# Sliding-window attention feeding a token mixer on one core: row sums for two steps, one predicated copy for two heads, and longer distances behind the scores

## The chip, the core and the metric

One core of a Trainium2 chip runs the whole kernel. The metric is the device time of one execution in microseconds (us). Engines are named as in the profile: PE (TensorE; its weight loads are PEld), DVE (VectorE), ACT (ScalarE), POOL (GpSimd) and SP (SyncE, which here only issues DMAs).

## The reference, cut to what matters

Three layers follow one another, on 4 batches of 768 tokens and 512 channels. The change lies in the first, attention with 8 heads of 64, 4 sink tokens and a window of 128:

```
scores = (q @ k.T) / 8                       # q, k, v: [4, 8, 768, 64]
keep   = (key < 4) or (0 <= query - key < 128)
a      = exp(scores - rowmax), 0 where not kept
a      = a / (sum(a) + 1e-9)
x      = a @ v                               # [4, 768, 512]
theta  = x @ w_theta
y      = w_tok_r @ (x cos theta) + w_tok_i @ (x sin theta)
u      = x + y;  u = u + relu(u @ w_ch)
out    = (sigmoid(causal 5-tap conv of u) * (u @ w_val)) @ w_out
```

## The kernel before, in words

**Tiling.** The queries are cut into blocks of 128 tokens: 6 a batch, 24 in all, here called groups (`g`, also `x` in the step functions; `i = g % 6` is the block within its batch). Heads go in pairs, 4 pairs to a block (`p`). One pair of one block is a step, `t = 4 g + p`, so there are `NT` = 96 steps. In the trace the eight score matmuls and weight loads of an even step belong to two steps, since `step_scores` issues steps `t` and `t + 1` together. A block needs only its own keys and the block's before, so the scores of a head are two pieces of 132 columns (128 keys and 4 sinks) in one PSUM bank.

**One step's way through the engines.** PE makes the scores (L428). DVE copies the keys of the block before over the masked half of the block's own (`copy_predicated`, L444, one for each head, none for the first block of a batch), then subtracts mask and takes the row maximum (L446, one for each head). ACT takes the exponential and the row sum (L452, one for each head). DVE adds eps to the two row sums of the step and inverts them (L461, L462), POOL multiplies the weights by that (L470). PE transposes the weights of two steps (L482, `weights_T`), ACT copies them out (L486), POOL cuts them by two triangles into the part for this block's values and the part for those of the block before (L493, L495). PE multiplies them with the values (L510, `attend`) and adds the sinks' part (L560, in `finish_x`). ACT copies the block's result to `uT` (L561) and rounds it to `xh` (L569); POOL makes the rest `xl` (L571); PE computes theta of the block from both (L101 to L103, 12 matmuls), and ACT copies it out (L584). The block's sink weights go a small way of their own (L526, L537, L543, L547, L551).

**The order** is written out by hand. The loop over `t` goes through the names of `ORDER` in each step; a name is a step function or a kind of deferred work that an earlier one put off with `later(kind, steps, f)`. What follows the scores does so at fixed distances:

```
LT, OX, OT = 4, 2 * NP, 4 * NP + 2        # NP = 4 head pairs
```

`LT` is how many steps after its scores a pair is transposed (`step_turn`), `OX` how many a block's `attend` and `finish_x` come after its first scores, `OT` the same for theta, half in each of two steps (`step_theta`). `split_x` comes 4 steps ahead of theta, and `keep_warm` issues a matmul on zeros in each step up to `OT`, which keeps PE occupied before theta begins. The loop ends `OT` steps after the last scores.

**Beside it run** the preparation of theta's weights (`wstages`, four blocks, one begun every four steps from step 0: DMA, ACT L133, POOL clamp L139, three joins on DVE L148, L151, L154, split by ACT L97 and POOL L98) and of the two token-mix matrices (12 jobs, one every 6 steps from step 18 on: the same operations, two transposes on DVE L236, and a DMA back to HBM). Keys and queries are loaded 8 steps ahead of a block's first scores; keys are transposed on PE 5 steps ahead, queries 4 (L393, copied out by ACT, L402). The first block of a batch also has its sink columns copied within `kT`, on DVE: `sink_keys(0)` (L410) and, a block later, `sink_keys(1)` (L412). The values of block `x` are loaded at step `4 x + TUNE['lv']` into one of three buffers, so that the load waits for `attend` of block `x - 2`. All DMAs are issued by SP, in order.

**PSUM** has 8 banks: `ps_s` (scores, four tiles of one bank, one for each head of two steps), `ps_t` 1, `ps_m` 2, `ps_h` 1 (`attend`, theta and keep-warm in turn).

After the last step the mixer's first steps (begun inside the last steps of the loop, at `turns`) go on with the token mix (L900 to L905), and then the channel layers (from L995) run to the end.

Of the kernel before, what the change touches and what calls it, by code (L numbers as in the profile page):

```python
# [9 lines left out]
F32 = mybir.dt.float32  # L10
# [4 lines left out]
ALU = mybir.AluOpType  # L15
AX = mybir.AxisListType
PSUM = bass.MemoryType.PSUM
DRAM = bass.MemoryType.DRAM

TUNE = dict(tc=0, xs=0, we=0, low=1, cut=1, xl=0, th=0, fx=0, nrm=0, w0=18, ll=8, lv=2, lq=4, lk=5, e=0, l2=0, ws=0, wp=4, bk=3, bq=3, bv=3, bqT=2, first=2, kw=4)  # L20
ORDER = ("range scale warm sinksT cut xl turn scores attend finish wth value wcopy scopy slow tcopy load "
         "softmax normalise low loads sink exp join sinks k sinkk q split theta qcopy fcopy thcopy fetch kcopy "
         "wturn ").split()
# [4 lines left out]
BIG = 3.0e38  # L28
# [7 lines left out]
def tile_sink_window_attention__then__token_mix__then__gated_conv(  # L36
# [16 lines left out]
    nc = tc.nc  # L53
    B, H, S, D = q.shape
    P = 128
    NP = H // 2
# [4 lines left out]
    SCALE = 1.0 / math.sqrt(D)  # L61
# [22 lines left out]
    th = {}  # L84
# [172 lines left out]
    def banded_attention(mixer):  # L257
        with ExitStack() as c0:
            pa = c0.enter_context(tc.tile_pool(name="pa", bufs=2))
            cq = c0.enter_context(ExitStack())  # L260
            pq = cq.enter_context(tc.tile_pool(name="pq", bufs=2, side="right"))
            ps_s = cq.enter_context(tc.tile_pool(name="ps_s", bufs=4, space=PSUM, side="right"))
            ps_t = c0.enter_context(tc.tile_pool(name="ps_t", bufs=1, space=PSUM))
            ps_m = c0.enter_context(tc.tile_pool(name="ps_m", bufs=2, space=PSUM))
            ps_h = c0.enter_context(tc.tile_pool(name="ps_h", bufs=1, space=PSUM))
# [1 line left out]
            ns = max(0, n_sink)  # L267
            ns += ns % 2
            KT = P + ns
            NR = 2 * NP * ns  # L270
            NSLOT = 3
            FIRST = TUNE['first']

# [8 lines left out]
            def later(kind, steps, f):  # L282
                defer.setdefault(kind, []).append((now[0] + steps, f))
# [16 lines left out]
            qn, kn, vn, qTs, vss, sms, pTs, sks, blks, xs, pss = ({} for _ in range(11))  # L300

            kT = pq.tile([P, NSLOT, NP, KT], F32, name="kT", bufs=1)
# [1 line left out]
            late = big.tile([P, 2, NQ * DM // 2], I32, tag=f"th{B - 1}", name="late")  # L304
            room = [late[:, z, :] for z in range(2)]
            bmask = pa.tile([96, NP], F32, name="bmask", bufs=1)
            eps = pa.tile([P, 2], F32, name="eps", bufs=1)
            nc.gpsimd.memset(eps, 1.0e-9)

            def build_masks():  # L310
# [39 lines left out]
            def load(g, what):  # L350
                b, i = divmod(g, NQ)
                for src, d, nm, bufs in ((k, kn, "kn", TUNE["bk"]), (q, qn, "qn", TUNE["bq"]), (v, vn, "vn", TUNE["bv"])):
                    if nm[0] not in what:
# [8 lines left out]
            def load_first(pieces):  # L362
                ts = []
                for src, d, nm in ((k, kn, "kn"), (q, qn, "qn")):
                    d[0] = pq.tile([P, H, D], F32, tag=nm, name=nm, bufs=TUNE["b" + nm[0]])
                    ts.append((d[0], src))
# [21 lines left out]
            def qk_transpose(g, which, p0=0, p1=NP):  # L388
# [5 lines left out]
                if which == 0:  # L394
                    if p0 == 0:
                        qTs[g] = pq.tile([P, NP, P], F32, tag="qT", name="qT", bufs=TUNE["bqT"])
                    d = qTs[g][:, p0:p1, :]
# [3 lines left out]
                def copies():  # L401
                    copier(TUNE['e'] >> which & 1)(d, ps)  # L402
                    if p1 == NP and which == 1 and i == 0 and ns:
# [3 lines left out]

            def sink_keys(n):
                if n == 0:
                    nc.vector.tensor_copy(kT[:, 0, :, P:KT], kT[:, 0, :, 0:ns])  # L410
                else:
                    nc.vector.tensor_copy(kT[:, 1:NSLOT, :, P:KT], kT[:, 0:1, :, P:KT]  # L412
                                          .to_broadcast([P, NSLOT - 1, NP, ns]))


            def scores(t):
                g, p = divmod(t, NP)
                i = g % NQ
                if i == 0:
                    w = 2 * P  # L420
                    k2 = kT[:, 0:1, p, 0:P].to_broadcast([P, 2, P])
                else:
                    o = (i - 1) % NSLOT
                    w = 2 * KT
                    k2 = kT[:, o:o + 2, p, :] if o < NSLOT - 1 else kT[:, 0:NSLOT:NSLOT - 1, p, :]
                pss[t] = [ps_s.tile([P, 512], F32, tag="s", name="ps_s") for _ in range(2)]
                for h, d in enumerate(halves):
                    nc.tensor.matmul(pss[t][h][:, 0:w], qTs[g][d, p, :], k2[d], start=True, stop=True)  # L428

            def softmax(t):  # L430
                g, p = divmod(t, NP)
                i = g % NQ
                if p == 0:
                    sms[g] = (pa.tile([P, 2, NP, ns + P], F32, tag="sm", name="sm"),
                              pa.tile([P, 2, NP], F32, tag="nm", name="nm"),
                              pa.tile([P, 2, NP], F32, tag="rs", name="rs"))
                sm, nm, rs = sms[g]
                a = ns if i == 0 else 0
                m = masks[min(i, 2)][:, a:]
                heads = list(enumerate(pss.pop(t)))  # L440
                if i > 0:
                    take = (upto if i % NSLOT == 0 else upper).bitcast(I32)
                    for h, ps in heads:
                        nc.vector.copy_predicated(ps[:, KT:KT + P], take, ps[:, 0:P])  # L444
                for h, ps in heads:
                    nc.vector.tensor_tensor_reduce(sm[:, h, p, a:], ps[:, P:KT + P - a], m, -SCALE, BIG, ALU.add,  # L446
                                                   ALU.min, nm[:, h, p:p + 1])

                def exps():
                    for h in range(2):  # L450
                        x = sm[:, h, p, a:]
                        nc.scalar.activation(x, x, AF.Exp, bias=nm[:, h, p:p + 1], scale=-1.0,  # L452
                                             accum_out=rs[:, h, p:p + 1])

                later("exp", 0, exps)

            def normalise(t):
                g, p = divmod(t, NP)
                sm, nm, rs = sms[g]
                r = rs[:, :, p]  # L460
                nc.vector.tensor_tensor(r, r, eps, ALU.add)  # L461
                nc.vector.reciprocal(r, r)  # L462
                x = sm[:, :, p, ns:]

                def scale():
                    if TUNE['nrm'] >> p & 1:
                        for h in range(2):
                            nc.vector.tensor_scalar(x[:, h], x[:, h], rs[:, h, p:p + 1], None, ALU.mult)
                    else:
                        nc.gpsimd.tensor_tensor(x, x, rs[:, :, p:p + 1].to_broadcast([P, 2, P]), ALU.mult)  # L470

                later("scale", 0, scale)

# [111 lines left out]


            NT = NG * NP
            LT, OX, OT = 4, 2 * NP, 4 * NP + 2  # L590
            W0, WP = TUNE['w0'], 6
            turns = [NT + n for n in (1, 4, 6, 7, 9)]
            load_first(FIRST)
# [62 lines left out]
                    softmax(t)  # L656

            def step_normalise(t, g, p):
                if 1 <= t <= NT:
                    normalise(t - 1)  # L660

            def step_sinks(t, g, p):
                if p == 0 and 1 <= g <= NG:
# [4 lines left out]
                    sink_T(g - 1)  # L668

            def step_attend(t, g, p):  # L670
                if OX <= t < NT + OX and t % NP == 0:
                    attend((t - OX) // NP)

            def step_finish(t, g, p):
# [66 lines left out]
            for t in range(NT + OT):  # L741
                now[0] = t
                g, p = divmod(t, NP)
# [388 lines left out]
```

## Time and profile before

| | us |
|---|---|
| median of 3 runs | 685.65 (684.75 to 686.59) |
| the profiled execution's own time | 688.93 |
| its span, first to last instruction | 687.2 |
| PE busy in the span | 658.7 (96%) |
| DVE busy | 522.0 (76%) |
| POOL busy | 402.9 (59%) |
| ACT busy | 356.5 (52%) |
| PE's weight loads busy | 578.0 (84%) |

Durations come from the profiled execution. The windows view gives the busy time of each engine in stretches of the span; the timeline gives single instructions with start, duration and, in brackets, how long the engine idled before and what ended that; "lines" groups instructions by line, engine and shape with busy time, mean duration and idle time before; the chain is the work that ended last, followed back from the end. Matmuls are pipelined and their ends are modelled, so that a busy PE isn't always PE at its peak. PEclk is the clock granted to TensorE as a share of 2.4 GHz.

### The profile page before, as it was taken

To read this page: it belongs to the slowest core of one execution; us is meant where nothing else is said; L and a number is where in the kernel's file an instruction comes from. 1 tells how busy PE (TensorE), PEld (TensorE's weight loads), DVE (VectorE), ACT (ScalarE), POOL (GpSimd) and SP (SyncE) were. 2 spreads that over 40 slices of the span, in tenths; PEclk is the share of its full clock that TensorE was granted. 3 is DMA by queue.
4 is the path that set the end of the run, shared out by engine and by line. 5 is a ranking of instruction groups with operands and counts; after the bars stand their busy time and mean duration, and the time that the engine had idled before them with its cause. 6 is when DMAs were issued, how large, how long until landed. Compare 5 with 4: busy or idle time off the path is not lost.

```text
span 687.2 us, 12293 instructions
## 1 busy us (share of the span) xinstructions
PE 658.7 (96%) x4139; PEld 578.0 (84%) x4139; DVE 522.0 (76%) x1409; ACT 356.5 (52%) x967; POOL 402.9 (59%) x457
## 2 busy tenths in 40 slices
PE   7779999999999999999999999999999999999998
PEld 4557767677677677999999999999989989989997
DVE  3686899989978965955656677676889889889773
ACT  5668777786777758643534444443423323323222
POOL 5588788879878885433433444436756447447330
PEclk9899999999999999999999999999999999999999
DMA  7747667797777246000110111100000100110111
GB/s 188 168 94 137 132 148 176 140 191 165 144 150 146 55 132 200 1 1 28 35 46 17 47 31 46 47 32 31 1 31 17 47 31 16 47 38 9 47 46 47
DMA packets 104334, 53.34 MB, mean 78 GB/s; under 512 B 80592, under 2 KB 96208, under 8 KB 104272
## 3 DMA queue, kind: packets, MB, share of 16 engines
q1 hardware_dynamic: 104272, 52.56, 31.7%
q8 instruction: 33, 0.54, 0.3%
q14 instruction: 29, 0.24, 0.1%
HBM read 41.54 MB, written 11.01 MB: 76 GB/s over the span
## 4 chain that ended last, share of the span: by engine, by line
PE 65%; DVE 21%; ACT 4%; POOL 3%; issue 3%; DMA 2%; SPq 1%; DVEq 0%; ACTq 0%; POOLq 0%
PE ps_y L103 9%; PE ps_y L101 9%; PE ps_y L102 9%; PE ps_s L428 3%; PE ps_o L103 3%; DVE acc L1043 3%; PE ps_o L102 3%; PE ps_o L101 3%; DVE sm L446 3%; DVE wc L154 2%; PE ps_c L103 2%; PE ps_c L101 2%; PE ps_c L102 2%; DVE ps_s L444 2%; PE ps_v L101 2%
## 5 line engine op out<-in xcount | busy, mean ns | idle before, releaser
L98 POOL TENSOR_TENSOR zl<-cs,zh 128x512 fp32r<-128x512 f32 x48 | 65.5, 1365 | 94.8 <-ACT zh L97 79.4
L1043 DVE SCALAR_TENSOR_TENSOR acc<-x,cw,acc 128x384 f32<-128x384 f32 x128 | 106.6, 833 | 2.4
L452 ACT ACTIVATE sm<-sm,nm 128x132 f32<-128x132 f32 (+1 forms) x192 | 76.3, 400 | 35.9 <-DVE nm L446 35.8
L470 POOL TENSOR_TENSOR sm<-sm,rs 128x256 f32<-128x256 f32 x96 | 69.7, 727 | 32.6 <-ACT sm L452 22.3
L98 POOL TENSOR_TENSOR x2l<-x,x2h 128x384 fp32r<-128x384 f32 x32 | 39.2, 1225 | 55.4 <-ACT x2h L97 55.4
L97 ACT CAST zh<-cs 128x512 fp32r<-128x512 f32 x48 | 29.8, 622 | 77.0 <-DVE cs L888 67.3
L428 PE MATMUL ps_s<-kT,qT 64*128 64x264 f32 (+1 forms) x384 | 63.4, 427 | 5.1 <-DVE nm L446 5.1
L101 PE MATMUL ps_y<-wt0h,zh 128*128 128x384 f32 x192 | 68.3, 356 | 0.0
L103 PE MATMUL ps_y<-wt0h,zl 128*128 128x384 f32 x192 | 64.9, 338 | 1.6 <-POOL zl L98 1.5
L103 PE MATMUL ps_y<-wt1h,zl 128*128 128x384 f32 x192 | 64.6, 337 | 0.0
L102 PE MATMUL ps_y<-wt1l,zh 128*128 128x384 f32 x192 | 64.6, 336 | 0.0
L102 PE MATMUL ps_y<-wt0l,zh 128*128 128x384 f32 x192 | 64.5, 336 | 0.0
L101 PE MATMUL ps_y<-wt1h,zh 128*128 128x384 f32 x192 | 64.5, 336 | 0.0
L428 PEld LDWEIGHTS ps_s<-kT,qT 64*128 64x128 f32 x384 | 36.2, 193 | 21.1 <-issue 8.3
L446 DVE CUSTOM_DVE_ANT_0 sm<-ps_s,mask 128x132 f32<-128x132 f32 (+1 forms) x192 | 48.4, 288 | 4.5 <-PE ps_s L428 3.9
L98 POOL TENSOR_TENSOR gl<-acc,gh 128x384 fp32r<-128x384 f32 x28 | 33.7, 1203 | 22.4 <-ACT gh L97 22.4
L444 DVE COPY_PREDICATED ps_s<-upper,ps_s 128x128 f32<-128x128 int32 x128 | 30.9, 287 | 19.7 <-PE ps_s L428 19.3
L97 ACT CAST x2h<-x 128x384 fp32r<-128x384 f32 x32 | 16.4, 514 | 54.7 <-DVE x L1029 54.7
L101 PE MATMUL ps_v<-x2h,held 128*128 128x384 f32 x128 | 43.3, 338 | 0.0
L102 PE MATMUL ps_v<-x2l,held 128*128 128x384 f32 x128 | 43.3, 338 | 0.0
L103 PE MATMUL ps_v<-x2h,held 128*128 128x384 f32 x128 | 43.2, 338 | 0.0
L101 PE MATMUL ps_h<-wthh,xh 128*128 128x512 f32 x96 | 42.3, 440 | 0.0
(157 smaller groups left out, 1978.6 us busy)
## 6 DMA issues: line engine op xcount, KB each, us to landing
vn<-in_v_dram SPq DMA_DIRECT2D x24, 256.0 KB, 4.7
kn<-in_k_dram SPq DMA_DIRECT2D x23, 256.0 KB, 4.6
qn<-in_q_dram SPq DMA_DIRECT2D x23, 256.0 KB, 5.1
out_dram<-o SPq DMA_DIRECT2D x23, 256.0 KB, 2.0
late<-in_moe_w_tok_r_dram SPq DMA_DIRECT2D x24, 192.0 KB
late<-in_moe_w_tok_i_dram SPq DMA_DIRECT2D x24, 192.0 KB, 3.2
wTr<-wTe SPq DMA_DIRECT2D x24, 96.0 KB, 3.6
wTi<-wTe SPq DMA_DIRECT2D x24, 96.0 KB, 2.8
```

The lines of the kernel that those rows point to most:

```text
L97: nc.scalar.copy(dst_h, src)
L98: lo_engine.tensor_tensor(dst_l, src, dst_h.bitcast(F32), ALU.subtract)
L101: nc.tensor.matmul(ps, lhs[0], rhs[0], start=first, stop=False)
L102: nc.tensor.matmul(ps, lhs[0], rhs[1], start=False, stop=False)
L103: nc.tensor.matmul(ps, lhs[1], rhs[0], start=False, stop=last)
L154: nc.vector.scalar_tensor_tensor(ci, lo, 29, ci, ALU.logical_shift_right, ALU.bitwise_or)
L428: nc.tensor.matmul(pss[t][h][:, 0:w], qTs[g][d, p, :], k2[d], start=True, stop=True)
L444: nc.vector.copy_predicated(ps[:, KT:KT + P], take, ps[:, 0:P])
L446: nc.vector.tensor_tensor_reduce(sm[:, h, p, a:], ps[:, P:KT + P - a], m, -SCALE, BIG, ALU.add, ALU.min, nm[:, h, p:p + 1])
L452: nc.scalar.activation(x, x, AF.Exp, bias=nm[:, h, p:p + 1], scale=-1.0, accum_out=rs[:, h, p:p + 1])
L470: nc.gpsimd.tensor_tensor(x, x, rs[:, :, p:p + 1].to_broadcast([P, 2, P]), ALU.mult)
L1043: nc.vector.scalar_tensor_tensor(a, x2[:, e, z:z + TB], cw[:, e, z:z + 1], a, ALU.mult, ALU.add)
```

## The change

The row sums of two steps are inverted in one pair of DVE operations on even steps, and their weights scaled by one POOL operation. The score tile holds both heads in two banks (two such tiles, as many banks as before), and one predicated copy serves both, with the mask broadcast over the heads. The sink columns are copied by ACT. `LT` goes from 4 to 6, `OX` from 8 to 10, `OT` from 18 to 20, and the values' load from 2 to 4 steps behind a block's first scores. As `OX` is no longer a multiple of 4, `attend` falls on the third step of a group, where it fell on the first; theta on the first and second, where it fell on the third and fourth.

```diff
-TUNE = dict(..., lv=2, ...)
+TUNE = dict(..., lv=4, ...)
...
-            ps_s = cq.enter_context(tc.tile_pool(name="ps_s", bufs=4, space=PSUM, side="right"))
+            ps_s = cq.enter_context(tc.tile_pool(name="ps_s", bufs=2, space=PSUM, side="right"))
...
-            eps = pa.tile([P, 2], F32, name="eps", bufs=1)
+            eps = pa.tile([P, 2, 2], F32, name="eps", bufs=1)
...
-                    nc.vector.tensor_copy(kT[:, 0, :, P:KT], kT[:, 0, :, 0:ns])
+                    nc.scalar.copy(kT[:, 0, :, P:KT], kT[:, 0, :, 0:ns])
                 else:
-                    nc.vector.tensor_copy(kT[:, 1:NSLOT, :, P:KT], kT[:, 0:1, :, P:KT]
+                    nc.scalar.copy(kT[:, 1:NSLOT, :, P:KT], kT[:, 0:1, :, P:KT]
                                           .to_broadcast([P, NSLOT - 1, NP, ns]))
...
-                pss[t] = [ps_s.tile([P, 512], F32, tag="s", name="ps_s") for _ in range(2)]
+                pss[t] = ps_s.tile([P, 2, 512], F32, tag="s", name="ps_s")
                 for h, d in enumerate(halves):
-                    nc.tensor.matmul(pss[t][h][:, 0:w], qTs[g][d, p, :], k2[d], start=True, stop=True)
+                    nc.tensor.matmul(pss[t][:, h, 0:w], qTs[g][d, p, :], k2[d], start=True, stop=True)
...
-                    for h, ps in heads:
-                        nc.vector.copy_predicated(ps[:, KT:KT + P], take, ps[:, 0:P])
-                for h, ps in heads:
-                    nc.vector.tensor_tensor_reduce(sm[:, h, p, a:], ps[:, P:KT + P - a], m, -SCALE, BIG, ALU.add,
+                    nc.vector.copy_predicated(ps[:, :, KT:KT + P], take[:, None, :].to_broadcast([P, 2, P]), ps[:, :, 0:P])
+                for h in range(2):
+                    nc.vector.tensor_tensor_reduce(sm[:, h, p, a:], ps[:, h, P:KT + P - a], m, -SCALE, BIG, ALU.add,
                                                    ALU.min, nm[:, h, p:p + 1])
...
-                r = rs[:, :, p]
+                r = rs[:, :, p:p + 2]
                 nc.vector.tensor_tensor(r, r, eps, ALU.add)
                 nc.vector.reciprocal(r, r)
-                x = sm[:, :, p, ns:]
...
-                        nc.gpsimd.tensor_tensor(x, x, rs[:, :, p:p + 1].to_broadcast([P, 2, P]), ALU.mult)
...
+                x = sm[:, :, p:p + 2, ns:]
+                later("scale", 0, lambda: nc.gpsimd.tensor_tensor(x, x, r[:, :, :, None].to_broadcast([P, 2, 2, P]),
+                                                                  ALU.mult))
...
-            LT, OX, OT = 4, 2 * NP, 4 * NP + 2
+            LT, OX, OT = 6, 2 * NP + 2, 5 * NP
...
-                if 1 <= t <= NT:
-                    normalise(t - 1)
+                if 2 <= t <= NT and t % 2 == 0:
+                    normalise(t - 2)
...
-                if OX <= t < NT + OX and t % NP == 0:
+                if OX <= t < NT + OX and (t - OX) % NP == 0:
                     attend((t - OX) // NP)
```

## Rows read from the trace of the kernel before

**Rows 1.** Windows: us; busy us of PE, PEld, DVE, ACT, POOL; PEclk, DMA share, GB/s

```profile
24.56:59.05 34.49, 26.58 (x204) 18.75 (x204) 22.89 (x108) 23.05 (x78) 26.51 (x37) 0.95 0.63 131
...
59.05:239.15 180.10, 172.63 (x1347) 131.03 (x1346) 159.06 (x629) 136.00 (x440) 146.82 (x193) 0.99 0.69 142
239.15:267.01 27.86, 26.42 (x197) 20.41 (x196) 17.41 (x52) 17.45 (x46) 20.20 (x26) 1.00 0.57 181
267.01:687.00 419.99, 414.66 (x2313) 397.49 (x2311) 311.20 (x556) 166.28 (x362) 196.97 (x166) 1.00 0.10 32
126.54:137.90 11.36, 11.36 (x89) 8.83 (x87) 10.85 (x37) 8.74 (x29) 10.25 (x14) 1.00 0.63 136
137.97:147.29 9.32, 9.32 (x78) 7.34 (x77) 7.87 (x32) 6.55 (x22) 6.54 (x8) 1.00 0.81 158
186.00:188.00 2.00, 2.00 (x7) 1.50 (x6) 1.88 (x9) 1.60 (x8) 1.93 (x4) 0.50 0.72 158
```

**Rows 2.** The chain of waits, PE's pieces: start us, us, what

```profile
53.72 0.44 PE ps_t L482 x4
...
248.90 1.97 PE ps_x L510 x32
250.86 0.43 PE ps_x L560
```

**Rows 3.** Timeline of the head, 40 to 47 us, engines in order of time

```profile
40.47 0.59 ACT L561 COPY uT<-ps_x 128x512 f32<-128x512 f32 x1
...
41.79 1.27 POOL L98 TENSOR_TENSOR wthl<-wc,wthh 128x512 fp32r<-128x512 f32 x1
43.03 0.61 POOL L139 TENSOR_SCALAR wc<-wc 128x512 f32<-128x512 f32 x1
...
43.68 0.83 DVE L148 TENSOR_SCALAR wc<-wc 128x512 int32<-128x512 int32 x1 [2.93 <-POOL wc L139]
...
46.72 0.44 PE L482 MATMUL ps_t<-ident,sm 128*128 128x128 f32 x2 [1.97 <-POOL sm L470]
```

**Rows 4.** Waits, 0 to 270 us: us in total, times, longest us

```profile
PEld ps_t L482 <- POOL sm L470: 11.4, 10, 2.2
```

**Rows 5.** Lines by shape, DVE, 0 to 270 us

```profile
L444 DVE COPY_PREDICATED ps_s<-upper,ps_s 128x128 f32<-128x128 int32 x128 | 30.9, 287 | 19.7 <-PE ps_s L428 19.3
L461 DVE TENSOR_TENSOR rs<-rs,eps 128x2 f32<-128x2 f32 x96 | 29.6, 308 | 1.9 <-ACT sm L452 1.9
...
L462 DVE RECIPROCAL rs<-rs 128x2 f32<-128x2 f32 x96 | 16.2, 168 | 3.3
...
L410 DVE COPY kT<-kT 128x16 f32<-128x16 f32 x4 | 5.8, 1453 | 0.5 <-ACT kT L402 0.5
...
L888 DVE TENSOR_TENSOR cs<-cs,ps_n 128x512 f32<-128x512 f32 x2 | 1.4, 688 | 1.2 <-ACT cs L881 1.2
```

**Rows 6.** Timeline, DVE: two predicated copies, and two of the sink copies

```profile
118.45 0.46 DVE L444 COPY_PREDICATED ps_s<-upper,ps_s 128x128 f32<-128x128 int32 x2
...
120.10 2.74 DVE L410 COPY kT<-kT 128x16 f32<-128x16 f32 x1
...
180.34 2.74 DVE L410 COPY kT<-kT 128x16 f32<-128x16 f32 x1
```

**Rows 7.** Lines by shape, ACT and POOL

```profile
L543 ACT CAST skr<-ps_sk 96x128 fp32r<-96x128 f32 x20 | 5.0, 248 | 0.0
...
L571 POOL TENSOR_TENSOR xl<-uT,xh 128x512 fp32r<-128x512 f32 x18 | 22.9, 1273 | 0.0
```

**Rows 8.** The row sums' tile: duration ns least/median/most, first and last start

```profile
L461 DVE TENSOR_TENSOR rs<-rs,eps x96: 150/160/1182, 12.1 to 248.2; 128x2 f32<-128x2 f32 x96
...
L470 POOL TENSOR_TENSOR sm<-sm,rs x96: 605/616/1274, 12.6 to 251.2; 128x256 f32<-128x256 f32 x96
```

**Rows 9.** Timeline: the load of a block's keys on SP, its transposes on PE

```profile
138.07 0.49 SPq L360 DMA_DIRECT2D kn<-in_k_dram  x1
...
145.46 0.60 PE L393 MATMUL ps_qk<-ident,kn 128*128 128x128 f32 x4
```

**Rows 10.** DMA issues, 40 to 260 us: KB each, median us to landing

```profile
kn<-in_k_dram SPq DMA_DIRECT2D x18, 256.0 KB, 5.9
```

More of the change, by code (lines that the diff above doesn't have):

```diff
@@ L18 @@
 DRAM = bass.MemoryType.DRAM
-TUNE = dict(tc=0, xs=0, we=0, low=1, cut=1, xl=0, th=0, fx=0, nrm=0, w0=18, ll=8, lv=2, lq=4, lk=5, e=0, l2=0, ws=0, wp=4, bk=3, bq=3, bv=3, bqT=2, first=2, kw=4)
+TUNE = dict(tc=0, xs=0, we=0, low=1, cut=1, xl=0, th=0, fx=0, nrm=0, w0=18, ll=8, lv=4, lq=4, lk=5, e=0, l2=0, ws=0, wp=4, bk=3, bq=3, bv=3, bqT=2, first=2, kw=4)
 ORDER = ("range scale warm sinksT cut xl turn scores attend finish wth value wcopy scopy slow tcopy load "
@@ L439, in softmax @@
                 m = masks[min(i, 2)][:, a:]
-                heads = list(enumerate(pss.pop(t)))
+                ps = pss.pop(t)
                 if i > 0:
                     take = (upto if i % NSLOT == 0 else upper).bitcast(I32)
-                    for h, ps in heads:
-                        nc.vector.copy_predicated(ps[:, KT:KT + P], take, ps[:, 0:P])
-                for h, ps in heads:
-                    nc.vector.tensor_tensor_reduce(sm[:, h, p, a:], ps[:, P:KT + P - a], m, -SCALE, BIG, ALU.add,
+                    nc.vector.copy_predicated(ps[:, :, KT:KT + P], take[:, None, :].to_broadcast([P, 2, P]), ps[:, :, 0:P])
+                for h in range(2):
+                    nc.vector.tensor_tensor_reduce(sm[:, h, p, a:], ps[:, h, P:KT + P - a], m, -SCALE, BIG, ALU.add,
                                                    ALU.min, nm[:, h, p:p + 1])
@@ L459, in normalise @@
                 sm, nm, rs = sms[g]
-                r = rs[:, :, p]
+                r = rs[:, :, p:p + 2]
                 nc.vector.tensor_tensor(r, r, eps, ALU.add)
                 nc.vector.reciprocal(r, r)
-                x = sm[:, :, p, ns:]
[L465 to L469, printed above, removed]
-                        nc.gpsimd.tensor_tensor(x, x, rs[:, :, p:p + 1].to_broadcast([P, 2, P]), ALU.mult)
-                later("scale", 0, scale)
+                x = sm[:, :, p:p + 2, ns:]
+                later("scale", 0, lambda: nc.gpsimd.tensor_tensor(x, x, r[:, :, :, None].to_broadcast([P, 2, 2, P]),
+                                                                  ALU.mult))
             def weights_T(t):
```

## The prediction

> **What bounds the kernel now.** Start with the stretches of the windows view [rows 1]. From 267.01 us to the end TensorE (PE) is busy 414.66 of 419.99 us. The change touches nothing there, so its effect lies in the attention stage, 0 to 267 us. In the 18 groups whose scores open at 59.05 and 239.15 us, PE is busy 172.63 of 180.10 us, VectorE (DVE) 159.06, GpSimd (POOL) 146.82, ScalarE (ACT) 136.00. A group (four steps) takes 180.10/18 = 10.0 us there, and DVE works 159.06/18 = 8.84 us of it.
>
> Two stretches show what these means mix. From 137.97 to 147.29 PE has no gap: 9.32 of 9.32 us, DVE 7.87. That is PE's own time for a full group. From 126.54 to 137.90 a group takes 11.36 us with DVE at 10.85: there DVE sets the pace, and PE's "busy" is stretched by waiting. So PE and DVE take turns. If nothing but PE held the 18 groups they would need 18 x 9.32 = 167.8 us, less three groups that open a batch: 16 of 32 attention matmuls and one sink matmul fewer, about 1.97/2 + 0.43 = 1.4 us each by the chain's pieces [rows 2]. That is 163.6 us; what there is to gain here ends at 16.5 us.
>
> The head is another case. From 24.56 to 59.05 three groups take 34.49 us, 11.5 each, while PE is busy 26.58/3 = 8.86 and POOL 26.51/3 = 8.84 a group [rows 1]. No engine is full; a chain goes round [rows 3]: the copy of `uT` at 40.47 (ACT, behind the attention matmuls), the split of `wthl` at 41.79 and the clamp at 43.03 (POOL), L148 at 43.68 after DVE idled 2.93 us, softmax, and the second half of the weights' transposes (L482) at 46.72, after PE idled 1.97 us for POOL's scaling. The next scores follow at once. Over the stage PE's weight loads for L482 stood 11.4 us in 10 waits for POOL's L470 [rows 4].
>
> **Part by part.** *Row sums of two steps at once.* L461 and L462 go from 96 to 48 each. Their busy time is 29.6 + 16.2 = 45.8 us for 96 [rows 5], so 48 fewer take 22.9 us off DVE, 0.95 a group. The row sum is four numbers a partition, not two; I price that at nothing, since the mean of 308 ns is start-up and waiting.
>
> *One predicated copy for two heads.* L444 mean 287 ns, but two in a row take 0.46 us together, because they overlap [rows 6]. One of 256 elements isn't in the trace. From below: the PSUM-reading L888 takes 688 ns for 512 elements, so (688 - 287)/384 = 1.04 ns an element, and 287 + 128 x 1.04 = 421 ns. From above: two copies without overlap, 574 ns. I take 421, the same kind of PSUM read: 80 x (0.46 - 0.42) = 3 us off DVE; by the upper end 9 us onto it. The shared two-bank score tile frees both heads together, one reduction (0.29 us) later than the first head alone; the ring still holds two steps, so I cost that at nothing while DVE is ahead.
>
> *Sink columns to ACT.* L410 takes 5.8 us of DVE in four copies (L412, four more, is left out of the sum) [rows 5]; two of them, as at 120.10 and 180.34, ran 2.74 us for 16 columns [rows 6]. ACT gets the eight small copies, nearest row 248 ns [rows 7]: 2 us on an engine with 44 us free of 180. Soon after the copy at 180.34, from 186 to 188, PE's granted clock is 0.50, the lower level of 1.2 GHz [rows 1]; a stretch at half clock costs PE up to half of its length.
>
> *One scaling for two steps.* L470 from 96 to 48, on 512 columns. Its median for 256 is 616 ns [rows 8], a 512-column operation takes 1273 [rows 7]: 2 x 616 = 1232, so POOL neither gains nor loses. DVE sheds 22.9 + 3 + 5.8 = 32 us in all, about 1.4 a group: 8.84 goes to 7.45, under the 7.87 at which PE ran without a gap.
>
> Against this stands a rule. L461 has a mean of 308 ns and a median of 160 [rows 5, 8]: some stand much longer than their work, 96 x 0.148 = 14 us in all. The Trainium skill ("SBUF — State Buffer", Who interferes with whom) says that VectorE and GpSimd share a port pair, an exclusive lock held for a whole instruction. By it a scaling twice as long blocks up to twice as long, so that the 7 us of this that I count as gone could all stay on DVE, and 32 would be 25. The forecast keeps 32 and would be the same with 25 (0.3 us a group): the slack of 9.32 - 7.45 us holds it.
>
> *Distances 4, 8, 18 to 6, 10, 20.* A pair's scaling is now issued on step 3 after its first scores and transposed on step 6: three steps between them where there was one. The L482 wait goes. Attention matmuls move from a group's first step to its third, theta from third and fourth to first and second. So in the head the `uT` copy no longer stands ahead of ACT's split of theta's weights, and the chain above opens in two places. What is late next there is POOL (8.84) or PE (8.86). I take 9.4, half a microsecond above, for what rest the joins leave: 34.49 - 3 x 9.4 = 6.3 us off. The keep-warm matmuls run two steps longer, in time that PE idles. For the 18 groups I take 9.4 each, as three groups are short but joins still bunch: 180.1 - 169.2 = 10.9 us off.
>
> After the last scores PE has one attention group (1.97 + 0.43) and a set of transposes (0.44) more [rows 2]: 2.8 us. The stretch from 239.15 to 267.01 has 27.86 - 26.42 = 1.4 us without PE [rows 1]; data that come two steps sooner should fill 1.0. That gives 1.8 back. The mixing's first steps keep their places.
>
> *Queues.* On SyncE (SP) the value load moves from two steps after its group's first scores to four, and there stands directly ahead of the next keys' and queries' loads. It waits for attention matmuls that also moved by two, so the wait isn't longer; behind it are keys, queries and the token weights' fetches. POOL keeps its order.
>
> Sum: -6.3 - 10.9 + 1.8 = -15.4 us. The profiled execution took 688.93 us (span 687.2), 3.28 above the median of 685.65; 673.5 for it becomes 670.2 for the median.
>
> **Rivals.** *A, only the stalls go (19%).* If the head stays on POOL because `wthl`, clamp and cuts are still in one queue, and DVE's joins keep bunching, then what is sure is the two long sink copies (2.74 us each less some 0.25) and the spell of low clock behind one of them, 5 to 8 us: 679.
>
> *B, DVE was the bound all along (8%).* DVE's 88% and PE's weight loads at 131.03 of 180.10 (73%) speak for it [rows 1]; the gapless group at 9.32 speaks against. If PE's pipeline had that room, DVE's whole 32 us would come off: about 654. The Trainium skill's "Perfetto Trace Analysis" (Identifying the Most-Contended Engine) says just this, that matmul busy time misleads and weight-load share should be read; the trace agrees on the shares, not yet on the bound.
>
> *C, slower: the keys land late (7%).* Keys issued at 138.07 are transposed at 145.46, 7.4 us on; they land in a median of 5.9, a margin of 1.5 [rows 9, 10]. The lead shrinks with the groups to 7.4 x 9.4/10 = 7.0, and a value load directly ahead takes up to 0.256 MB / 142 GB/s = 1.8 us. Then keys come 0.7 us late, PE's queue stands in all of some 20 groups, and 14 us eat the gain. From 0.8 us late it decides, at 1.0 the kernel is at 690. Against it: other groups have leads of 8 us and more, as loads run ahead.
>
> *D, nothing to measure (6%).* The gain and the longer drain cancel: 685.
>
> **Numbers.** The forecast (60%) covers 663 to 677: the copy's upper end and groups at 9.6 make it smaller, groups at 9.2 and a head at 8.9 larger. The range that holds 8 in 10 goes from 659 (towards B) to 681 (A). A measurement of this kernel can tell 0.3%, 2 us. Forecast, A and B are faster: 0.87; D is same: 0.06; C slower: 0.07.
>
> **What would show it.** Right: L444 x80 near 420 ns; L461 x48; L482's wait for L470 gone; L148's wait for the clamp under 1 us; score openings from the sixth group to the last about 169 us apart; DVE under 80% there; no 0.5 clock after the head. Wrong: PE waiting for `kn` (C), head groups above 10.5 us (A), groups well under 9.3 (B), L444 above 550 ns.

## The result, and the profile after

The changed kernel takes 669.47 us, the median of four runs (668.57 to 671.25), against 685.2 (684.14 to 686.59) for the kernel before in the same session: a ratio of 0.9759, 95% interval 0.9737 to 0.9781 (the quotient of these two medians, 0.977, lies within it). The forecast was 670.0, between 659 and 681.

In the code after, line numbers are smaller: L444 is now L443, L446 L445, L452 L451, L461 and L462 are L460 and L461, L470 is L463, L482 is L474, L493 and L495 are L485 and L487, L510 is L502, L561 is L553.

First the page's line of busy time. DVE goes from 522.0 to 485.5 us and POOL from 402.9 to 394.5, while the work of PE is the same. Of its 10 us less some 3 can be the clock (an estimate from the mean granted clock of the two executions, 0.992 before and 0.997 after); the rest I put down to time in which it was called busy and waited.

```profile
PE 648.7 (97%) x4141; PEld 573.3 (86%) x4141; DVE 485.5 (73%) x1226; ACT 355.2 (53%) x975; POOL 394.5 (59%) x408
```

Then the windows view of the profile after, in the stretches of [rows 1] (us; busy us of PE, PEld, DVE, ACT, POOL; PEclk, DMA share, GB/s): the head, the 18 groups, the drain up to the first mixing matmul, and the mixing to the end.

```profile
22.30:53.16 30.86, 24.05 (x193) 16.46 (x194) 18.63 (x88) 22.32 (x78) 23.38 (x29) 0.94 0.61 135
53.16:218.64 165.48, 164.87 (x1348) 127.65 (x1347) 130.79 (x491) 135.08 (x446) 141.86 (x157) 1.00 0.77 156
218.64:250.80 32.16, 29.40 (x213) 22.99 (x212) 17.52 (x48) 21.02 (x53) 24.20 (x26) 1.00 0.52 164
250.80:668.50 417.70, 413.90 (x2313) 397.63 (x2311) 308.18 (x554) 163.64 (x357) 194.46 (x165) 1.00 0.10 32
```

In the 18 groups PE now has 0.61 us without work, where it had 7.47, and a group takes 9.19 us on the mean; DVE's share there fell from 88% to 79%. By stage, from the openings (first score matmul) of the groups:

| us | before | after | difference | forecast |
|---|---|---|---|---|
| start to opening of the first group | 6.5 | 7.0 | +0.5 | 0 |
| first two groups | 18.0 | 15.3 | -2.7 | 0 |
| head, three groups | 34.5 | 30.9 | -3.6 | -6.3 |
| 18 groups | 180.1 | 165.5 | -14.6 | -10.9 |
| last opening to first mixing matmul | 27.9 | 32.2 | +4.3 | +1.8 |
| mixing to the end | 420.2 | 417.8 | -2.4 | 0 |
| span | 687.2 | 668.6 | -18.6 | -15.4 |

These are the two profiled executions, and the one before ran 3.3 us above its median, the one after 0.9. Part of what separates them is the clock and not the schedule: granted were 0.91 in the first two groups before and 1.00 after, and 0.99 and 1.00 in the 18 groups.

The lines by shape of the profile after (busy us, mean ns, idle time before), up to 250 us: of DVE, then of POOL and of ACT, cut to what answers to [rows 5], [rows 7] and [rows 8].

```profile
L443 DVE COPY_PREDICATED ps_s<-upper,ps_s 128x256 f32<-128x256 int32 x64 | 27.0, 422 | 31.7 <-PE ps_s L428 31.3
L460 DVE TENSOR_TENSOR rs<-rs,eps 128x4 f32<-128x4 f32 x48 | 22.1, 461 | 1.5 <-ACT sm L451 1.5
...
L154 DVE SCALAR_TENSOR_TENSOR wc<-late,wc 128x768 int32<-128x768 int32 x12 | 15.2, 1270 | 0.0
...
L461 DVE RECIPROCAL rs<-rs 128x4 f32<-128x4 f32 x48 | 8.6, 179 | 1.7
```

```profile
L463 POOL TENSOR_TENSOR sm<-sm,rs 128x512 f32<-128x512 f32 x48 | 55.9, 1164 | 18.1 <-ACT sm L451 8.2 <-DVE rs L461 5.4 <-PE ps_x L502 4.6
```

```profile
L410 ACT COPY kT<-kT 128x16 f32<-128x16 f32 x4 | 0.8, 210 | 0.0
```

The copy for two heads takes 422 ns (421 forecast). DVE now idles 31.3 us ahead of it, waiting for PE's scores: DVE is ahead of PE, as wanted. The row sums take 22.1 + 8.6 = 30.7 us for 45.8, a saving of 15.1 and not of 22.9, since each row sum stands 461 ns where it stood 308. POOL's scaling fell from 96 x 727 ns = 69.7 us to 55.9. The waits view of the stage (us in total, times, longest) still has two that stand mostly in the head (6.5 of the 10.0 us below lie in its three groups, the rest before it), and L474's wait for POOL's scaling, 11.4 us in ten waits of the weight loads before [rows 4], is not among them any more:

```profile
DVE wc L148 <- POOL wc L139: 10.0, 4, 3.8
PE ps_warm L592 <- ACT uT L553: 5.9, 3, 2.7
```

### The profile page after: what moved, and what is told of

Read it like the earlier page. It is cut to its first block, busy times and chain, and to the rows that moved or that the text cites. A ratio compares the mean times of both kernels' runs of the same rounds, so it can differ in the third digit from the quotient of the medians.

```text
span 668.6 us, 11958 instructions
## 1 busy us (share of the span) xinstructions
PE 648.7 (97%) x4141; PEld 573.3 (86%) x4141; DVE 485.5 (73%) x1226; ACT 355.2 (53%) x975; POOL 394.5 (59%) x408
## 4 chain that ended last, share of the span: by engine, by line
PE 82%; DVE 8%; issue 3%; ACT 2%; POOL 2%; DMA 1%; SPq 1%; DVEq 0%; ACTq 0%; POOLq 0%
PE ps_y L103 10%; PE ps_y L101 10%; PE ps_y L102 10%; PE ps_s L428 6%; PE ps_x L502 5%; PE ps_o L103 3%; DVE acc L1035 3%; PE ps_o L102 3%; PE ps_o L101 3%; PE ps_h L101 3%; PE ps_qk L393 3%; PE ps_h L103 3%; PE ps_h L102 3%; PE ps_c L103 2%; PE ps_c L101 2%
## 5 line engine op out<-in xcount | busy, mean ns | idle before, releaser
L451 ACT ACTIVATE sm<-sm,nm 128x132 f32<-128x132 f32 (+1 forms) x192 | 76.2, 400 | 29.0 <-DVE nm L445 28.8
L463 POOL TENSOR_TENSOR sm<-sm,rs 128x512 f32<-128x512 f32 x48 | 55.9, 1164 | 18.1 <-ACT sm L451 8.2
L428 PE MATMUL ps_s<-kT,qT 64*128 64x264 f32 (+1 forms) x384 | 59.8, 423 | 4.1 <-DVE nm L445 3.1
L445 DVE CUSTOM_DVE_ANT_0 sm<-ps_s,mask 128x132 f32<-128x132 f32 (+1 forms) x192 | 48.9, 292 | 9.9 <-PE ps_s L428 5.0
L428 PEld LDWEIGHTS ps_s<-kT,qT 64*128 64x128 f32 x384 | 33.3, 191 | 19.6 <-issue 8.6
L443 DVE COPY_PREDICATED ps_s<-upper,ps_s 128x256 f32<-128x256 int32 x64 | 27.0, 422 | 31.7 <-PE ps_s L428 31.3
L880 DVE TENSOR_TENSOR cs<-cs,ps_n 128x512 f32<-128x512 f32 x48 | 32.7, 681 | 11.5 <-ACT cs L873 10.2
```

The lines of the kernel that those rows point to most:

```text
L428: nc.tensor.matmul(pss[t][:, h, 0:w], qTs[g][d, p, :], k2[d], start=True, stop=True)
L445: nc.vector.tensor_tensor_reduce(sm[:, h, p, a:], ps[:, h, P:KT + P - a], m, -SCALE, BIG, ALU.add, ALU.min, nm[:, h, p:p + 1])
L463: later("scale", 0, lambda: nc.gpsimd.tensor_tensor(x, x, r[:, :, :, None].to_broadcast([P, 2, 2, P]), ALU.mult))
L880: nc.vector.tensor_tensor(x, x, pn[:, None, :].to_broadcast([P, 2, HD]), ALU.mult)
```

## The experiments

Every run is given as its median and as its ratio to the kernel before on the same chip; ratios are what is compared. "The change" is the whole one at 0.9759.

### The parts alone: distances, row sums, sinks

**The distances alone**, in the kernel before:

```diff
-TUNE = dict(..., lv=2, ...)
+TUNE = dict(..., lv=4, ...)
...
-            LT, OX, OT = 4, 2 * NP, 4 * NP + 2
+            LT, OX, OT = 6, 2 * NP + 2, 5 * NP
...
-                if OX <= t < NT + OX and t % NP == 0:
+                if OX <= t < NT + OX and (t - OX) % NP == 0:
```

> The kernel before with distances 6, 10, 20 and the value load 4 steps behind, and nothing else changed: DVE keeps its 32 us. My theory: head about 4 us less, the 18 groups about 4 us less (no wait for POOL's scaling), the drain 4 us more: 678 to 683. If the distances did all of it: 668 to 671. If DVE's load did all of it: 685 to 689, the longer drain showing alone.

Measured: 677.44 us, 0.9878 (0.9860 to 0.9897), just under the range and about half of the gain. Waits of L482 for the scaling are no longer listed. The 18 groups take 172.2 us with DVE busy for 155.2 of them.

**The row sums alone**, with the scaling that belongs to them, in the kernel before:

```diff
-                r = rs[:, :, p]
+                r = rs[:, :, p:p + 2]
...
-                x = sm[:, :, p, ns:]
+                x = sm[:, :, p:p + 2, ns:]
...
-                if 1 <= t <= NT:
-                    normalise(t - 1)
+                if 2 <= t <= NT and t % 2 == 0:
+                    normalise(t - 2)
```

> The kernel before with row sums, reciprocal and scaling merged over two steps, at the old distances, and nothing else changed. DVE loses about 20 us of work, but the scaling of a pair, now of 1.05 us, stands one step ahead of its transposes. My theory: 3 to 7 us less, 678 to 682, with PE's wait for POOL's scaling larger than the 11.4 us of before. Rival (DVE's load was the bound): 670 to 674. Rival (the pair's scaling comes too late for the old distance): 686 or more.

Measured: 687.23 us, 1.0016 (1.0000 to 1.0031), as the second rival had it. DVE was relieved as hoped: row sums and reciprocals take 15.5 + 8.6 = 24.1 us for 45.8. The time did not move, since the relief came back elsewhere. The waits view of this kernel (us in total, times, longest):

```profile
PEld ps_t L482 <- POOL sm L470: 23.3, 23, 2.7
PE ps_t L482 <- POOL sm L470: 16.7, 16, 2.3
```

The first was 11.4 us in ten waits before [rows 4]. The first of the two steps now waits for the second before it is scaled, and a transpose four steps behind the scores comes too early for that.

**The change with the old distances**:

```diff
-TUNE = dict(..., lv=4, ...)
+TUNE = dict(..., lv=2, ...)
...
-            LT, OX, OT = 6, 2 * NP + 2, 5 * NP
+            LT, OX, OT = 4, 2 * NP, 4 * NP + 2
```

> The changed kernel with distances 4, 8, 18 and the value load 2 steps behind, as before; merged row sums, two-head copy and sink columns on ACT stay. My theory (DVE and the short distances both held the stage; each part gives some, the head's chain needs the distances): the 18 groups gain about 8 us, the head nothing, the drain does not grow: 676 to 680. If the distances did all of it: 684 to 686. If DVE's load did all of it: 668 to 671.

Measured: 689.2 us, 1.0042 (1.0019 to 1.0065): slower than before, which neither theory had. The waits view shows the same turn as in the run above:

```profile
PEld ps_t L474 <- POOL sm L463: 22.5, 21, 2.9
PE ps_t L474 <- POOL sm L463: 17.3, 15, 2.5
```

DVE was busy for only 126.73 of the 179.06 us of the 18 groups, less than in the changed kernel, and still they took as long as before. So it was not DVE's load alone that held them.

**The sinks alone**, in the kernel before:

```diff
-                    nc.vector.tensor_copy(kT[:, 0, :, P:KT], kT[:, 0, :, 0:ns])
+                    nc.scalar.copy(kT[:, 0, :, P:KT], kT[:, 0, :, 0:ns])
...
-                    nc.vector.tensor_copy(kT[:, 1:NSLOT, :, P:KT], kT[:, 0:1, :, P:KT]
+                    nc.scalar.copy(kT[:, 1:NSLOT, :, P:KT], kT[:, 0:1, :, P:KT]
```

> The kernel before with the sink columns copied by ACT and nothing else changed. My theory: the two copies of 2.74 us go, and with one of them the half-clock stretch near 186 us: 3 to 6 us less, 679 to 682. Rival (the long copies only stood where DVE would have waited for scores anyway): 684 to 686.

Measured: 683.85 us, 0.9958 (0.9943 to 0.9974), just under 3 us; the 18 groups go from 180.1 to 177.2. That is less than forecast, between the theory and the rival. Both copies of 2.74 us [rows 6] are gone, and the two groups they stood in, 12.97 and 11.38 us long before, take 10.20 and 10.23. The stretch at the lower clock behind the second is gone with it: granted is 1.00 over the 18 groups of this run.

**The change without merged row sums** (copy, sinks and distances stay):

```diff
-                r = rs[:, :, p:p + 2]
+                r = rs[:, :, p]
...
-                x = sm[:, :, p:p + 2, ns:]
+                x = sm[:, :, p, ns:]
...
-                if 2 <= t <= NT and t % 2 == 0:
-                    normalise(t - 2)
+                if 1 <= t <= NT:
+                    normalise(t - 1)
```

> The changed kernel with the row sums, the reciprocal and the scaling of every step by themselves again (96 of each, not 48); the one copy for two heads, the sink columns on ScalarE and the longer distances stay. Theory: with the distances in place the merged row sums pay what VectorE sheds by them, half or more of the 8 us that lie between the distances alone (677.4 us) and the whole change (669.5): 673.5 to 677. Rival 1: the two-head copy and the sinks bring all of it, the merge nothing: 669 to 671. Rival 2: the merge costs here too, as it did without the distances: under 668.5.

Measured: 680.89 us, 0.9914 (0.9901 to 0.9928), beyond every range: it is slower than the distances alone (0.9878). With the distances in place the merge is worth 0.9914 - 0.9759 = 1.55% of 685 us, 10.6 us, and the two-head copy and the sinks together, without the merge, cost some 2.5 us. In the windows view the 18 groups of the distances alone (first) and of this kernel (second) have almost the same DVE time, though the second has 6 us fewer copies, the sinks' among them, by the sum of its lines:

```profile
53.37:225.61 172.24, 168.14 (x1348) 129.36 (x1347) 155.18 (x625) 134.35 (x440) 147.90 (x193) 1.00 0.74 150
```

```profile
55.73:229.79 174.06, 167.77 (x1348) 127.11 (x1347) 154.12 (x560) 135.27 (x446) 147.76 (x193) 1.00 0.73 149
```

Two copies in a row overlapped before [rows 6], so that merging them takes little off the union. What costs the 2.5 us was not separated; that the shared score tile frees both heads only together is a guess.

The four corners (the copy and the sinks are in the three runs marked *):

| ratio to before | row sums of each step | row sums of two steps |
|---|---|---|
| distances 4, 8, 18 | 1 | 1.0016, and 1.0042* |
| distances 6, 10, 20 | 0.9878, and 0.9914* | 0.9759* |

The merge brings nothing at the old distances (no run separates the 1.0042 into its parts) and 10 us at the new ones, measured there with the copy and the sinks in place; distances and merge without these two were not run. So the distances work alone in part, and the merge only with them.

### Who sets the pace now

**Twice the copy.** In the change each predicated copy is issued a second time, on the same data:

```diff
                     nc.vector.copy_predicated(ps[:, :, KT:KT + P], ...)
+                    nc.vector.copy_predicated(ps[:, :, KT:KT + P], ...)
```

> The changed kernel with each two-head predicated copy issued twice (the same result): 80 more of 0.35 to 0.42 us, 28 to 34 us more work for DVE, which brings it back to the load of before at the new distances. My theory (PE sets the pace now, DVE has some 20% to spare, of which joins that bunch need a part): 674 to 680, as with the distances alone. Rival B of the prediction (DVE is the bound): 695 or more. If DVE's time were free altogether: 669 to 671.

Measured: 686.02 us, 0.9996 (0.9978 to 1.0013): 16 us dearer than the change, between the two expectations. The added copies take 27.4 + 6.9 = 34.3 us of DVE, so about half of what is added shows. The 18 groups:

```profile
57.25:234.02 176.77, 168.37 (x1348) 126.74 (x1347) 149.33 (x551) 135.64 (x446) 140.08 (x158) 1.00 0.71 146
```

Here 18.5 us more DVE time in the window (149.33 for 130.79) make it 11.3 us longer (176.77 for 165.48). The new distances do not make DVE's load free: the slack of the changed kernel is small. The second copy stands in the way from the scores to the row maximum as well, and this run doesn't separate that delay from the load.

**Less work for PE.** Theta without its third product (12 matmuls a block become 8), in the change and in the kernel before:

```diff
-                mm3(hps[g], [x[:, c, :] for x in x2], [w[c] for w in wth], c == 0, c == KC - 1)
+                nc.tensor.matmul(hps[g], x2[0][:, c, :], wth[0][c], start=c == 0, stop=False)
+                nc.tensor.matmul(hps[g], x2[0][:, c, :], wth[1][c], start=False, stop=c == KC - 1)
```

> The changed kernel without the third product of theta (the rounding rest of x times theta's weights): 96 matmuls of 0.23 us fewer, 22 us of PE's time, 0.93 us a group. My theory (PE is the bound of the 18 groups and of the drain): 14 to 20 us less than the changed kernel, 650 to 656. Rival (a chain through DVE and POOL is the bound): 664 or more.

> The kernel before without the third product of theta: the same 22 us of PE's time. My theory (before, PE sets the pace only in part of the groups, the rest is DVE and waits for POOL): 5 to 11 us less than before, 674 to 680. Rival (PE was the bound before as well): 14 us or more less, under 671.

Measured: in the change 666.5 us, 0.9708 (0.9678 to 0.9737), 3 us less; in the kernel before 680.36 us, 0.9904 (0.9873 to 0.9936), 5.5 less as expected. The first is a miss, and lies in the rival's range: PE has about 13 us less to do in the 18 groups (151.73 busy for 164.87), and they are only 4.3 us shorter. In the kernel before (second line) they are 4.6 us shorter, 175.51 for 180.10.

```profile
53.21:214.38 161.17, 151.73 (x1276) 113.59 (x1275) 136.01 (x490) 134.16 (x446) 142.53 (x158) 1.00 0.78 160
...
57.46:232.97 175.51, 161.92 (x1276) 117.32 (x1275) 162.42 (x628) 135.20 (x442) 147.92 (x194) 0.99 0.71 147
```

So PE sets the pace in the changed kernel only to a depth of 4 us. What stands behind it was not found out: in this window DVE is busy for 84%, POOL for 88%, and PE waits 1.8 us for keys. And the pair doesn't show that PE bounds the change more than the kernel before, since the 18 groups give the same in both; what tells the two apart is PE's time without work there, 7.47 us before and 0.61 after. In this run more relief of PE alone brought little.

### The head

**Split and clamp of theta's weights on DVE.** The waits for L139 were put down to POOL's queue, where the clamp stands behind the scaling, two cuts and the split of the block before. In the change:

```diff
-                w_clamp(job[1], nc.gpsimd)
+                w_clamp(job[1], nc.vector)
...
-            split(dst[0][c], dst[1][c], job[1][0], nc.gpsimd)
+            split(dst[0][c], dst[1][c], job[1][0], nc.vector if room is not None else nc.gpsimd)
```

> The changed kernel with the clamp and the rounding rest of theta's weights (four blocks, in the head) on DVE, not on POOL. My theory (in the head DVE still waits about 10 us for the clamp behind that split in POOL's queue, while DVE is busy 60%): the head's three groups shrink by 2 to 4 us, 665 to 668. Rival (the head is set by ACT behind PE's attention matmuls): 669 to 671. Rival (the split delays the softmax on DVE): 672 or more.

Measured: 676.47 us, 0.9855 (0.9824 to 0.9886), 6.6 us slower than the change, in the range of the second rival; the first two groups take 18.6 us for 15.3, the head 34.2 for 30.9, the 18 groups 165.5 as before. The timeline, DVE and ACT around one of the splits:

```profile
38.33 0.62 ACT L97 CAST wthh<-wc 128x512 fp32r<-128x512 f32 x1
...
38.98 1.14 DVE L98 TENSOR_TENSOR wthl<-wc,wthh 128x512 fp32r<-128x512 f32 x1 [1.50 <-ACT wthh L97]
40.04 0.85 DVE L139 TENSOR_SCALAR wc<-wc 128x512 f32<-128x512 f32 x1
40.81 0.41 DVE L443 COPY_PREDICATED ps_s<-upto,ps_s 128x256 f32<-128x256 int32 x1
```

The wait moved with the work: DVE now stands for ACT's rounding, and the softmax (L443) stands behind it. A faster engine for the clamp did not help; that it is the order in the queue is what the next run tests, with the engines left as they are.

**The joins one step later.** The clamp stays on POOL, and in the head one step without work is put between it and DVE's first join:

```diff
-        return [fetch, bits, join(0), join(1), join(2), parts]
+        return [fetch, bits] + [lambda: None] * light + [join(0), join(1), join(2), parts]
```

> The changed kernel, with one idle step between the clamp of theta's head weights and VectorE's first join while only a few groups run (the head). Theory: in the head VectorE stands about 10 us in four waits for the clamp, because the clamp lies behind the scaling and the cuts in GpSimd's queue; a join issued one step later lets the softmax of that step pass ahead of it, so the head gives 2 to 5 us back: 665 to 668 us against 669.5. Rival 1: the chain of the head then waits for theta itself or for the joins a step later, and the time stays: 669 to 671. Rival 2: joins bunch with the next group's, and the head gets longer: above 671.

Measured: 666.27 us, 0.9706 (0.9693 to 0.9719): a hit, and faster than the change with no overlap of the intervals. The windows and the waits of this kernel:

```profile
22.43:49.78 27.35, 22.63 (x193) 15.49 (x193) 22.02 (x88) 22.45 (x78) 22.98 (x28) 1.00 0.67 152
49.78:215.28 165.50, 164.69 (x1348) 127.66 (x1347) 131.02 (x491) 135.14 (x446) 142.19 (x158) 1.00 0.76 157
```

```profile
PE ps_qk L393 <- DMA kn<-in_k_dram: 3.9, 5, 2.9
PE ps_warm L592 <- ACT uT L553: 2.6, 3, 1.2
DVE wc L148 <- POOL wc L139: 2.0, 1, 2.0
```

The head is 3.5 us shorter with the same work, the wait for the clamp went from 10.0 to 2.0 us, and the 18 groups stay as they were. The granted clock in the head is 1.00 where it was 0.94, but that isn't the cause: the run with both edits, below, has 0.94 again and the same head, and among runs with a granted clock of 1.000 the change takes 668.6 us and this kernel 666.0. Of the 3.9 us for which PE waits for keys one wait of 2.9 lies ahead of the head.

**Keep-warm only up to the first attention matmuls.** A keep-warm matmul shares its bank with the sum that ACT copies to `uT`:

```diff
-                if t < OT + 1:
+                if t < OX:
```

> The changed kernel with its keep-warm matmuls only up to the step of the first attention matmuls, not up to the first output matmuls. Theory: in the head TensorE stands 2.5 and 2.7 us in its queue because a keep-warm matmul shares its output bank with the transposes that ScalarE still copies into uT; without it the head gives 1 to 4 us back: 665.5 to 668.5 us against 669.5. Rival 1: the next real instruction stands in the same place, for the same copy: 669 to 671. Rival 2: TensorE falls to the 0.5 clock in the gap and the scores behind it run at half speed: 671 to 675.

Measured: 668.62 us, 0.9740 (0.9726 to 0.9754), not told apart from the change: the intervals overlap, and the head takes 30.7 us for 30.9. The clamp's wait is the same 10.0 us, and with the later joins alone PE's stop behind the `uT` copy went from 5.9 to 2.6 us by itself: more than half of it hung on the first wait. The granted clock of the head is lower, 0.89, so the theory fell and the second rival showed in part.

**Both edits of the head:**

> The changed kernel with both edits of the head: the idle step ahead of the joins and the shorter keep-warm. Theory: two different waits of one stage, each of which can hide the other, so that the two together give at least the sum: 662 to 666 us against 669.5. Rival 1: one of them was the other's shadow, and the time is that of the better edit alone. Rival 2: the head is held by GpSimd's own work and nothing moves: 669 to 671.

Measured: 665.81 us, 0.9701 (0.9687 to 0.9714). The theory's range held the time, but its reason did not: the head takes 27.4 us, as with the later joins alone (at a granted clock of 0.94), and the intervals of the two overlap. It is the first rival: the one edit gives all. The later joins are the version to keep.

## Why the prediction was right, and where its terms were wrong

The forecast's own case happened, at 669.5 for 670.0. That it came so close is luck: errors of several us in its terms cancelled, and between the two profiled executions, on the first of which the sum was made, the gain was 18.6 us for 15.4.

**PE and DVE take turns, and PE's gapless group is what is left: held.** The 18 groups now run at 9.19 us each with 0.61 us of gaps in all; the floor worked out was 163.6 us, the stage took 165.5. In the slow group before, where DVE was busy for 10.85 us, that was not all its own work: L154 took 2.72 us there, at 130.81, and 0.94 at 85.33; it ran beside a row of POOL's operations, of which the section on DVE's relief has more. I had taken 9.4 a group for bunching joins; it is 3.7 us better (165.5 for 169.2). How near the next limit stands, some 4 us behind PE, the prediction did not see.

**"The L482 wait goes": held, and it was the distances that took it.** This carries more than I wrote. I costed the merged row sums and the distances as two savings that add up. By the runs the merge by itself is worth nothing (1.0016), since it doubles the very wait that the distances remove. DVE's relief counts only where PE is not waiting for the scaling.

**DVE's relief: the size held, the lines did not.** In the 18 groups DVE went from 159.06 to 130.79 us, 7.27 a group for the 7.45 forecast. Row sums gave 15.1 us over the stage for 22.9. What I had not counted made up for it: DVE's three joins of weights (L148, L151, L154, those of 768 columns) went from 48.8 to 37.5 us. Either half of the change does that alone, 38.5 with the merged row sums and 40.4 with the distances.

The term that was mis-sized is the time for which a row sum stands beyond its own work. The views of the tile `rs` (least, median, most in ns), of the merge alone, the distances alone and the change:

```profile
L461 DVE TENSOR_TENSOR rs<-rs,eps x48: 151/160/901, 13.4 to 246.9; 128x4 f32<-128x4 f32 x48
...
L461 DVE TENSOR_TENSOR rs<-rs,eps x96: 150/402/1072, 12.2 to 236.3; 128x2 f32<-128x2 f32 x96
...
L460 DVE TENSOR_TENSOR rs<-rs,eps x48: 157/350/1257, 13.5 to 229.0; 128x4 f32<-128x4 f32 x48
```

A row sum that nothing holds takes 160 ns. What goes beyond that:

| | row sums | us in all | beyond 160 ns each |
|---|---|---|---|
| before | 96 | 29.6 | 14.2 |
| the merge alone | 48 | 15.5 | 7.8 |
| the distances alone | 96 | 37.7 | 22.3 |
| the change | 48 | 22.1 | 14.4 |

So the merge does take off the 7 us that I counted as gone, although the scaling is longer, and the new distances put 7 to 8 us on. The timeline shows why. Of the 48 row sums of the change 28 take over 200 ns, and each of these ends within 0.03 us of the end of the POOL operation that ran when it began: 16 times `xl` (L563), 11 times `blk` (L543), once the split of theta's weights, never the scaling. One of them:

```profile
68.19 1.28 POOL L563 TENSOR_TENSOR xl<-uT,xh 128x512 fp32r<-128x512 f32 x1
...
68.64 0.85 DVE L460 TENSOR_TENSOR rs<-rs,eps 128x4 f32<-128x4 f32 x1
```

Before, 39 of 40 end so, but only four of them behind `xl` and six behind the scaling. The rule weighed there said that a scaling twice as long could hold the row sums up to twice as long; instead it counts which of POOL's operations a row sum meets. This agrees with the lock between the two engines of which the Trainium skill tells ("SBUF — State Buffer", Who interferes with whom), without the doubling that I had worked out from it.

**POOL "neither gains nor loses": wrong, by 13.8 us of its busy time.** I took the nearest 512-column row, 1273 ns, which writes another type; the scaling's median is 1047 ns, for 2 x 616 of two halves.

**The head: the step that failed.** "The chain above opens in two places" was right for the first, L482, and half right for the second: `uT` no longer stands ahead of the split's rounding, but L148's wait for the clamp, forecast under 1 us, stayed at 10.0 (11.0 before). The timeline of POOL and DVE after shows why:

```profile
35.02 1.04 POOL L463 TENSOR_TENSOR sm<-sm,rs 128x512 f32<-128x512 f32 x1
...
36.02 0.64 POOL L485 TENSOR_SCALAR_AFFINE_SELECT pp<-pc 128x512 f32<-128x512 f32 x1
...
36.72 0.64 POOL L487 TENSOR_SCALAR_AFFINE_SELECT pc<-pc 128x512 f32<-128x512 f32 x1
...
37.33 1.27 POOL L98 TENSOR_TENSOR wthl<-wc,wthh 128x512 fp32r<-128x512 f32 x1
...
38.58 0.61 POOL L139 TENSOR_SCALAR wc<-wc 128x512 f32<-128x512 f32 x1
...
39.22 0.43 DVE L148 TENSOR_SCALAR wc<-wc 128x512 int32<-128x512 int32 x1 [3.77 <-POOL wc L139]
39.56 0.42 DVE L443 COPY_PREDICATED ps_s<-upto,ps_s 128x256 f32<-128x256 int32 x1
```

Five operations without a gap, from 35.02 to 39.19, and DVE's softmax in line behind the join that needs the last one. I named POOL as what is late next but priced it by its busy time a group (8.84); its order was what counted. The experiment with later joins gives what the step had promised: 27.35 us for the forecast 28.2.

**The drain: mis-sized, and given back.** +4.3 us for +1.8: I had let data that come sooner fill 1.0 of the 1.4 us of gaps, while the gaps grew, from 27.86 - 26.42 = 1.4 us to 32.16 - 29.40 = 2.8. Priced at nothing were the mixing's first steps, which get 2.4 us shorter beside the longer drain, in every run with the new distances and the whole of theta (417.7 to 417.8 us), and the first two groups, 2.7 us shorter. One wait of 2.0 us of L482 for the scaling was there too, and so was a stretch at the lower clock (0.91 granted before, 1.00 after); the two were not separated.

**The rivals.** A (only the stalls go) fell for the 18 groups and was half right for the head. B (DVE was the bound all along) fell: at the old distances DVE's relief brings nothing, and now PE runs almost without a gap; that DVE stands close behind, the doubled copy shows. The rule beside it ("Perfetto Trace Analysis", Identifying the Most-Contended Engine, in the Trainium skill), to judge by weight loads and not by matmul busy time, would still leave PE a quarter of headroom in the 18 groups (127.65 of 165.48 us, 77%). Taking PE work away shortened them by 4.3 us, so PE was the bound there, though only just. C (keys late) did not come: PE waits 0.2 us for `kn` after, where it waited 1.1 before; it begins to show only with the later joins, 3.9 us. D (nothing to measure) fell with the gain.

## What to carry to other kernels

Merging two small operations makes the first one's result later by a step: look whether its consumer is so far behind that it does not notice, and move the consumer in the same edit, or the saving on the engine turns into a wait of the same size. Where engines take turns, price an edit only together with the wait that hides it, and try each half alone. And where an engine waits for another that is not full, read the order in that engine's queue: moving the waiting instruction a step later brought some 3 us, moving the work to the waiting engine cost 6.6.

## What the runs showed that was not expected

A small DVE operation can stand several times its own work without any semaphore: the row sum of 128 x 4 numbers took from 157 to 1257 ns, and the copy of 16 columns that took 2.74 us on DVE twice [rows 6] takes 210 ns on ACT. With the distances alone, still on DVE, it took 155 ns. The two long ones began while POOL ran and ended with the fifth of five POOL operations that followed one another with hardly a gap; for the one at 180.34, which ends at 183.08, the fifth is

```profile
182.41 0.65 POOL L493 TENSOR_SCALAR_AFFINE_SELECT pp<-pc 128x512 f32<-128x512 f32 x1
```

The L154 of 2.72 us at 130.81 began and stood beside such a row of POOL's operations as well. So hold a small DVE operation that takes long against POOL's operations beside it first.

One POOL operation on 512 columns of f32 takes 1047 ns where two on 256 take 1232, a saving of 15% for joining them.

In the head after, a stretch at the lower clock follows a stop of PE. Windows of two us:

```profile
40.00:42.00 2.00, 0.24 (x2) 0.16 (x2) 1.89 (x9) 1.35 (x5) 1.00 (x1) 1.00 1.04 234
42.00:44.00 2.00, 2.00 (x14) 1.49 (x14) 1.40 (x6) 1.45 (x6) 1.93 (x4) 0.72 0.99 165
44.00:46.00 2.00, 2.00 (x11) 1.22 (x8) 1.28 (x8) 0.86 (x4) 0.94 (x1) 0.50 0.57 110
```

PE worked 0.24 us of the first two, behind the `uT` copy that waited for the late softmax; then 0.50, the level of 1.2 GHz, while it is full. With the later joins the stop is shorter, and the head keeps 1.00; that run has its stretch at the lower clock earlier, in the first two groups.
